# A chunked attention whose instruction order is planned in the kernel, with 16x16 blocks inverted on VectorE and merged on TensorE

## The chip, the cores and the metric

The kernel runs on one core of one Trainium2 chip. The metric is device time in microseconds (us) of one execution. TensorE (PE in the profile) multiplies matrices, VectorE (DVE), ScalarE (ACT) and GpSimd (POOL) work on elements, and SyncE (SP) only issues transfers (DMAs). Each of these takes its own instructions strictly in the order in which the program lists them.

## The reference

The first half is a linear attention with a state per batch and head; the second is a mixture of eight experts on its output.

```python
def _attn_ref(r, k, v, w, a, b):          # each 4 x 8 x 768 x 40 (batch, head, time, channel)
    for t in range(S):
        y[:, :, t] = einsum('bhd,bhde->bhe', rt, state)
        Sa = einsum('bhde,bhe->bhd', state, at)
        state = state * wt[:, :, None, :] - einsum('bhd,bhe->bhde', Sa, bt) + einsum('bhd,bhe->bhde', vt, kt)

def _moe_ref(x, w_gate, w1, w2):          # x = y as 3072 tokens x 320
    P = exp(x @ w_gate - max); eight rounds of normalising rows and columns of P
    out = sum over the 8 experts e of P[:, e] * (relu(x @ w1[e]) @ w2[e])
```

## The kernel before

**Attention.** Time is cut into 12 chunks `c` of 64 steps; `b` is the batch, and the eight heads stand as four pairs (`NP = 4`). There are 48 (chunk, batch) pairs. For each there is a *preparation* (`prep`), which does not depend on the state: two scans on VectorE (`q` L123, `gf` L133), products with them on GpSimd (`kb` L147, `ab` L153 and L154), the matrix of the chunk's inner products on TensorE (`ll` L159), a transpose (`kt` L167), and copies into a set of operands (`sx`, `bb`, `cc`; 20 sets, named `sx` or `st` in the profile).

Then a 64x64 unit triangular matrix per head must be *inverted*. The negated lower part of `ll` goes to DRAM (`ld`) and comes back with one (batch, head, half) on each partition (`load_lu`, L360). Two chunks make a group, so 128 matrices of 32x32 stand on the 128 partitions. VectorE inverts their 8x8 diagonal blocks by rows (`inv_diag`, L184 and L187) and then doubles the block twice, from 8 to 16 and from 16 to 32 (`inv_off` and `contract`: a multiply at L193 and a reduction at L196). `finish` writes the 32x32 inverses to DRAM, `tload` brings them back with the right layout, and `tmat` joins two 32x32 inverses to the 64x64 inverse `tt` with two products on TensorE (`gp` L241, `op` L246).

The *step* (`recur`) is the part that runs through time: for each (c, b) the products `av` (L268), `xc` (two halves, L276), `pu` with `tt` (L287), `c2` (L294; named `c` in the profile), between them the masks and sums on VectorE (`f` L269, `pm` L289, `ws` L296) and copies on ScalarE, then the new state `z` (L311), its transpose `zt` (L316), and the output `y` on GpSimd (L300), which goes to DRAM as `xd`, and to the router as `lp` (L326) and `lg` (L330). A chunk's step of batch b needs the state of the chunk before; the four batches are independent of each other.

**Order.** The function sorts a list of events `(time, function)` with hand-set times (`SKEW`, `P0`, `PD`, `INV_DT`) and writes the code in that order; a scheduler that simulates a timeline then places the instructions of each engine. It does so for the experts' first blocks too, up to `N_MAN = 8`; from there the written order holds.

**Experts.** Each block multiplies 384 tokens with a quarter of an expert's first layer by a seven-product scheme (`product`, L564) and then its second layer (L629). Before the first block, `prep_w` must split and combine the weights (GpSimd and ScalarE) and `prep_x` the tokens read back from `xd` (`xs`; VectorE `xt` L536 to L541, `xcl` and `xch` L544 to L552). The first block needs three `prep_x` units.

Of the kernel before, what the change touches and what calls it, by code (L numbers as in the profile page):

```python
# [3 lines left out]

# [25 lines left out]
def attention(ctx, tc, d, xd, ps, pq, pt, gs, lg):  # L30
    nc = tc.nc
    pin = ctx.enter_context(tc.tile_pool(name="a_in", bufs=1))
    inv = ctx.enter_context(tc.tile_pool(name="a_inv", bufs=1))
# [30 lines left out]
    tt_b = [const.tile([128, 4 * NP, 128], F32, name=f"tt{i}") for i in range(NTB)]
    td_b = [const.tile([128, 4 * NP + 1, 32], F32, name="td")]
    lg_b = [const.tile([128, 4 * NP, 64], F32, name="lg")]
    ab_b = [pin.tile([128, NP, 128], F32, name=f"ab{i}") for i in range(2)]
    kb1 = pin.tile([128, NP, 2, 64], F32, name="kb")
    f_b = [const.tile([128, NP, 2, 104], F32, name=f"f{i}") for i in range(NFB)]
    rb_b = [io.tile([128, NP, 128], F32, name=f"rb{i}") for i in range(NRB)]  # L70
    x1_b = [const.tile([128, NP, 128], F32, name=f"x1{i}") for i in range(2)]
    g1_b = [pin.tile([RP, NP, 65], F32, name=f"g1{i}") for i in range(1)]
    vz_b = [const.tile([128, NP, 104], F32, name=f"vz{i}") for i in range(5)]
    c1_b = [const.tile([R2, NP, 104], F32, name=f"c1{i}") for i in range(2)]
    unf = inv.tile([128, 1056], F32, name="un")
    luf = inv.tile([128, 1056], F32, name="lu")
    prf = inv.tile([128, 2048], F32, name="pr")
    gtf = inv.tile([128, 256], F32, name="gt")
    un, lu, tn = (t[:, 0:1024].rearrange("u (a b) -> u a b", b=32) for t in (unf, luf, prf))
    und, lud = (t.rearrange("u (b x) -> u b x", x=264)[:, :, 0:256].rearrange("u b (c j) -> u b c j", j=32)  # L80
                for t in (unf, luf))
    for t in g1_b + ab_b:
        nc.vector.memset(t, 0.0)

    def clear():
        nc.gpsimd.memset(unf, 0.0)
        nc.gpsimd.memset(unf[:, 0:1024:33], 1.0)
        for t in vz_b + c1_b + lg_b:
            nc.vector.memset(t, 0.0)
        for t in rb_b + f_b:  # L90
            nc.vector.memset(t[96:128], 0.0)
        nc.vector.memset(td_b[0][:, 4 * NP], 0.0)
        for t in x1_b:
            nc.vector.memset(t[:, :, 104:128], 0.0)
        nc.vector.memset(kb1[96:128], 0.0)
        for t in tt_b:
            nc.gpsimd.memset(t, 0.0)
    fresh = set(range(NSX))

    def first_use(i):  # L100
        if i in fresh:
            fresh.discard(i)
            nc.gpsimd.memset(bb_b[i], 0.0)
            nc.scalar.copy(out=sx_b[i][64:128].rearrange("r p h x -> r (p h) x")[:, :, 64:104],
                           in_=cst[64:128, 360:400].unsqueeze(1).broadcast_to([64, 8, 40]))

    state = {"sx": 0, "ab": 0, "g1": 0, "vz": 0, "c1": 0, "tt": 0, "f": 0, "rb": 0, "x1": 0}

    def rot(key, lst):
        i = state[key]  # L110
        state[key] = (i + 1) % len(lst)
        return lst[i]

    zp = [None] * NB

    def prep(c, b, ld):
        cb = c * NB + b
        inp = raws[IN_MAP[cb]][0:RP, 0:1029] if IN_MAP.get(cb) else pin.tile([RP, 1029], F32, name="inp", bufs=2)
        nc.sync.dma_start(out=inp, in_=d["inp"][c, b])
        kb_in = inp[0:R2, 261:773].rearrange("r (p k t) -> r p k t", p=NP, k=2)  # L120
        a_in = inp[0:R2, 773:1029].rearrange("r (p t) -> r p t", p=NP)
        qf = pin.tile([RP, NP, 65], F32, name="q")
        nc.vector.tensor_tensor_scan(  # L123
            out=qf.rearrange("r p t -> r (p t)"), data0=inp[:, 0:260], data1=one65,
            initial=0.0, op0=ALU.mult, op1=ALU.add)
        q = qf[0:R2]
        g1 = rot("g1", g1_b)
        nc.vector.reciprocal(out=g1[:, :, 64], in_=qf[:, :, 64])
        sx = rot("sx", sx_b)
        i = next(j for j in range(NSX) if sx_b[j] is sx)  # L130
        bb, cc = bb_b[i], cc_b[i]
        gf = pin.tile([RP, NP, 65], F32, name="gf", bufs=2)
        nc.vector.tensor_tensor_scan(  # L133
            out=gf.rearrange("r p t -> r (p t)")[:, 259::-1], data0=inp[:, 260:0:-1],
            data1=g1.rearrange("r p t -> r (p t)")[:, 259::-1], initial=0.0, op0=ALU.mult, op1=ALU.add)
        gd[c, b] = dr1.tile([RP, 260], F32, name=f"gd{cb}")
        nc.sync.dma_start(out=gd[c, b], in_=gf.rearrange("r p t -> r (p t)"))
        g = gf[0:R2, :, 64:0:-1]
        if cb < NKB:
            raw = raws[KB_SETS[cb % len(KB_SETS)]]  # L140
            kb = raw[0:R2, 0:512].rearrange("r (p k t) -> r p k t", p=NP, k=2)
            lt = raw[0:64, 512:1024].rearrange("r (p k t) -> r p k t", p=NP, k=2)
        else:
            kb = kb1
            lt = pin.tile([64, NP, 2, 64], F32, name="lt")
        eng = nc.vector if cb < NFAST else nc.gpsimd
        (nc.gpsimd if cb in KB_POOL else eng).tensor_tensor(  # L147
            out=kb[0:R2], in0=kb_in,
            in1=q[:, :, 63::-1].unsqueeze(2).broadcast_to([R2, NP, 2, 64]), op=ALU.mult)
        ab = rot("ab", ab_b)  # L150
        first_use(i)
        nc.gpsimd.tensor_copy(out=cc, in_=q[:, :, 64])
        eng.tensor_tensor(out=ab[0:40, :, 0:64], in0=a_in[0:40], in1=g[0:40], op=ALU.mult)  # L153
        eng.tensor_tensor(out=ab[64:104, :, 64:128], in0=a_in[64:104], in1=g[64:104], op=ALU.mult)  # L154
        nc.scalar.copy(out=sx[64:128, :, 0, 0:64], in_=ab[0:64, :, 0:64])
        nc.scalar.copy(out=sx[64:128, :, 1, 0:64], in_=ab[64:128, :, 64:128])
        ll = pq.tile([128, NP, 2, 64], F32, name="ll", tag="pq")
        for p in range(NP):
            nc.tensor.matmul(ll[:, p], lhsT=kb[:, p], rhs=ab[0:kb.shape[0], p], start=True, stop=True)  # L159
        if cb < NKB:  # L160
            nc.scalar.activation(out=lt, in_=ll[64:128], func=AF.Copy, scale=-1.0)
            (nc.sync if cb < N_SP else nc.scalar).dma_start(out=ld[GRP[c][1], :, b], in_=lt)
            kt = pt.tile([128, NP, 2, 64], F32, name="kt", tag="pt")
        else:
            kt = pq.tile([128, NP, 2, 64], F32, name="kt", tag="pq")
        for p in range(NP):
            nc.tensor.transpose(kt[:, p].rearrange("s h x -> s (h x)")[:, 0:R2],  # L167
                                kb[0:R2, p].rearrange("r k s -> r (k s)"), ident[0:R2, 0:R2])
        nc.vector.tensor_tensor(
            out=sx[0:64, :, :, 0:64], in0=ll[0:64],  # L170
            in1=mask_u.unsqueeze(1).unsqueeze(1).broadcast_to([64, NP, 2, 64]), op=ALU.mult)
        if cb >= NKB:
            nc.scalar.activation(out=lt, in_=ll[64:128], func=AF.Copy, scale=-1.0)
# [646 lines left out]
```

## Time and profile before

| | us |
|---|---|
| three runs: median (lowest to highest) | 1845.69 (1838.58 to 1847.31) |
| the profiled execution | 1846.42 |
| its span, first to last instruction | 1844.6 |
| TensorE busy in the span | 1717.9 |
| VectorE busy | 1395.4 |
| GpSimd busy | 882.4 |
| ScalarE busy | 855.9 |

The profile's rows give for each group of instructions the line in the kernel, the engine, the tiles written and read, the shape, the number of instructions, and busy time and mean. A float32 matmul shows as two records, a transpose as one. Matmuls are pipelined, so what a burst of them costs TensorE is read from one burst's start to the next one's start. The span has two stages: the attention up to about 520 us, and the experts from there.

### The profile page before, as it was taken

How to read it: one execution, taken by the hardware profiler on the slowest of the kernel's cores; microseconds unless marked ns; L12 is line 12 of the kernel's file. 1: busy time of each engine (PE TensorE's matmuls, PEld its weight loads, DVE VectorE, ACT ScalarE, POOL GpSimd, SP SyncE). 2: the span in 40 equal slices, each digit the busy share in tenths (PEclk: the TensorE clock that was granted, in tenths of full speed). 3: DMA queues.
4: the chain of work that ended last, by engine and by line, in shares of the span. 5: the costliest groups of instructions: out<-in, count | busy, mean ns of one | idle time of the engine just before them, and what ended most of it. 6: DMA issues, size and time to landing. Idle time of an engine off the chain costs nothing.

```text
span 1844.6 us, 31499 instructions
## 1 busy us (share of the span) xinstructions
PE 1717.9 (93%) x11843; PEld 1684.3 (91%) x11843; DVE 1395.4 (76%) x2315; ACT 855.9 (46%) x1848; POOL 882.4 (48%) x848
## 2 busy tenths in 40 slices
PE   4478898888989999999999999999999999999999
PEld 4368788888878999999999999999999999999999
DVE  7877979777598868677776868977686877767675
ACT  6357576675643534344343433445343443425342
POOL 6545655441573618355371826007191744628170
PEclk8579899999999999999999999999999999999999
DMA  8477787885730102011110202201020111102001
GB/s 211 117 169 160 175 201 178 178 179 129 188 95 31 56 2 74 21 55 38 38 56 19 75 20 68 66 12 57 20 75 20 56 38 38 57 19 75 5 34 43
DMA packets 194957, 145.10 MB, mean 79 GB/s; under 512 B 143861, under 2 KB 171637, under 8 KB 194805
## 3 DMA queue, kind: packets, MB, share of 16 engines
q1 hardware_dynamic: 191125, 137.35, 28.6%
q10 hardware_dynamic: 3680, 5.74, 1.1%
q8 instruction: 94, 1.54, 0.4%
q14 instruction: 58, 0.48, 0.1%
HBM read 117.00 MB, written 26.04 MB: 78 GB/s over the span
## 4 chain that ended last, share of the span: by engine, by line
PE 72%; DVE 13%; DMA 4%; issue 3%; POOL 3%; ACT 1%; SPq 1%; DVEq 0%; ACTq 0%; POOLq 0%
PE op L629 36%; PE p L564 33%; DVE pr L193 2%; DVE gt L196 2%; DMA inp<-in_inp_dram 1%; DVE un L196 1%; DVE q L123 1%; POOL kb L147 1%; DVE gf L133 1%; PE xc L276 1%; PE ll L159 1%; DMA ld<-lt 1%; DMA xs<-xd 1%; POOL ab L154 1%; DVE sm L582 1%
## 5 line engine op out<-in xcount | busy, mean ns | idle before, releaser
L564 PE MATMUL p<-xch,wh 128*128 128x384 f32 (+1 forms) x1792 | 604.8, 339 | 9.5 <-DVE sm L582 5.6
L585 ACT ACTIVATE hh<-sm 128x384 fp32r<-128x384 f32 x512 | 269.4, 527 | 723.2 <-DVE sm L582 723.2
L629 PE MATMUL op<-wh,hh 128*128 128x320 f32 x1536 | 476.4, 311 | 1.0 <-ACT hh L585 0.9
L629 PE MATMUL op<-wl,hh 128*128 128x320 f32 x1536 | 474.2, 309 | 0.0
L629 PE MATMUL op<-wh,hl 128*128 128x320 f32 x1536 | 466.7, 309 | 0.8 <-DVE hl L588 0.8
L510 POOL TENSOR_TENSOR wl<-ws,wh 128x640 fp32r<-128x640 f32 x60 | 103.1, 1718 | 605.6 <-ACT wh L508 605.4
L588 DVE SCALAR_TENSOR_TENSOR hl<-sm,hh 128x384 fp32r<-128x384 f32 x512 | 373.4, 763 | 2.4 <-ACT hh L585 2.0
L564 PEld LDWEIGHTS p<-xch,wh 128*128 128x128 f32 (+1 forms) x1792 | 336.8, 188 | 13.7 <-DVE sm L582 6.8
L564 PE MATMUL p<-xcl,wh 128*128 128x384 f32 x896 | 302.2, 337 | 0.0
L564 PE MATMUL p<-xch,wl 128*128 128x384 f32 x896 | 301.5, 337 | 0.0
L629 PEld LDWEIGHTS op<-wh,hh 128*128 128x128 f32 x1536 | 289.9, 189 | 1.6 <-ACT hh L585 1.5
L629 PEld LDWEIGHTS op<-wl,hh 128*128 128x128 f32 x1536 | 290.7, 189 | 0.0
L629 PEld LDWEIGHTS op<-wh,hl 128*128 128x128 f32 x1536 | 286.4, 188 | 1.2 <-DVE hl L588 1.0
L582 DVE TENSOR_TENSOR sm<-p,u 128x384 f32<-128x384 f32 x384 | 233.0, 617 | 8.8
L582 DVE TENSOR_TENSOR sm<-p,p 128x384 f32<-128x384 f32 x128 | 71.3, 557 | 129.0 <-PE p L564 74.4
L564 PEld LDWEIGHTS p<-xcl,wh 128*128 128x128 f32 x896 | 168.4, 188 | 0.0
L564 PEld LDWEIGHTS p<-xch,wl 128*128 128x128 f32 x896 | 168.4, 188 | 0.0
L582 DVE TENSOR_TENSOR p<-p,p 128x384 f32<-128x384 f32 x128 | 71.1, 556 | 101.6 <-PE p L564 101.2
L582 DVE TENSOR_TENSOR u<-p,p 128x384 f32<-128x384 f32 x128 | 70.8, 553 | 57.2 <-PE p L564 56.0
L159 PE MATMUL ll<-ab,kb 128*128 128x128 f32 x336 | 60.8, 335 | 48.3 <-POOL ab L154 23.2
L518 POOL TENSOR_TENSOR wl<-ss,wh 128x512 fp32r<-128x512 f32 x60 | 89.7, 1495 | 30.1 <-ACT wh L515 25.9
L159 PEld LDWEIGHTS ll<-ab,kb 128*128 128x128 f32 x336 | 52.3, 237 | 54.1 <-POOL kb L147 27.2
(161 smaller groups left out, 2747.3 us busy)
## 6 DMA issues: line engine op xcount, KB each, us to landing
ws<-in_wts_dram SPq DMA_DIRECT2D x60, 832.0 KB
inp<-in_inp_dram SPq DMA_DIRECT2D x42, 450.2 KB
rb<-in_r_dram SPq DMA_DIRECT2D x48, 224.0 KB
gd<-gf SPq DMA_DIRECT2D x48, 113.8 KB
gr<-gd SPq DMA_DIRECT2D x48, 113.8 KB
vz<-in_v_dram SPq DMA_DIRECT2D x48, 112.0 KB
ld<-lt ACTq DMA_DIRECT2D x40, 128.0 KB
f<-in_vt_dram SPq DMA_DIRECT2D x48, 80.0 KB
```

Of the source, the lines that this page charges most:

```text
L123: nc.vector.tensor_tensor_scan(out=qf.rearrange("r p t -> r (p t)"), data0=inp[:, 0:260], data1=one65, initial=0.0, op0=ALU.mult, op1=ALU.add)
L133: nc.vector.tensor_tensor_scan(out=gf.rearrange("r p t -> r (p t)")[:, 259::-1], data0=inp[:, 260:0:-1], data1=g1.rearrange("r p t -> r (p ...
L159: nc.tensor.matmul(ll[:, p], lhsT=kb[:, p], rhs=ab[0:kb.shape[0], p], start=True, stop=True)
L193: nc.vector.tensor_tensor(out=prv, in0=a.unsqueeze(3).broadcast_to([nu, n_c, n_k, n_r]), in1=m.unsqueeze(1).broadcast_to([nu, n_c, n_k, n_ ...
L196: nc.vector.tensor_reduce(out=dst, in_=prv.rearrange("u c k r -> u c r k"), op=ALU.add, axis=AX.X)
L510: g.tensor_tensor(out=wl[:, 0:640], in0=raw[:, 256:896], in1=wh[:, 0:640], op=ALU.subtract)
L518: g.tensor_tensor(out=lv[:, 3:7], in0=so[:, :, 0], in1=hv[:, 3:7, 0], op=ALU.subtract)
L564: nc.tensor.matmul(o, lhsT=w_, rhs=x_, start=(j == 0), stop=(j == 3))
L582: eng.tensor_tensor(out=out, in0=x, in1=y, op=ALU.add)
L585: nc.scalar.activation(out=hh[:, f, h], in_=sm[f][:, h], func=AF.Relu)
L588: v.scalar_tensor_tensor(out=hl[:, f, h], in0=sm[f][:, h], scalar=0.0, in1=hh[:, f, h], op0=ALU.max, op1=ALU.subtract)
L629: nc.tensor.matmul(ops[i], lhsT=a[:, h, cs], rhs=w_[:, cw], start=(f == 0 and h == 0 and j == 0), stop=(last and h == 1 and j == 2))
```

## The change

1. **The order.** A class `Plan` collects every operation of the attention (on TensorE, VectorE, ScalarE, GpSimd and SyncE) with a duration, what it depends on, a due time, and the buffers that it takes and gives back. `order()` plays them through, engine by engine, always taking the ready operation with the earliest key, and the code is written in that order under a manual schedule. All eight PSUM banks become one pool. Transfers that ScalarE issued (`ld`) go to SyncE.
2. **The inversion.** VectorE stops at 16x16 blocks. Blocks are merged from 16 to 32 and from 32 to 64 on TensorE by products of 32-row tiles (`merge`: `mm_ga`, `mm_at`, `mm_tb`, `mm_gb`, `mm_tc`).
3. **The groups.** The first chunk is inverted alone; the groups are 1, 2, 2, 2, 2, 2, 1 chunks.
4. **The step.** `tt` is stored as two 64-wide halves and not as a block-diagonal 128x128 matrix, so `pu` and `c2` are two 64-row products for each pair of heads. `xd` has its rows in another order, which `_layout` follows.

The experts' code is the same.

```diff
+    def order(self):
+        ...
+                    busy[e] = o.end = t + d
+        ...
-GROUPS = [[0, 1], [2, 3], [4, 5], [6, 7], [8, 9], [10, 11]]
-NSX = 20
-T_LEAD = 2
+SIZES = dict(set=17, inp=3, q=2, gf=2, g1=2, kb=2, ab=2, lt=2, vz=5, rb=2, gr=2, f=3, x1=2, c1=2, pm=2, ws=2, y=2,
+             z=5, tt=2, inv=1, m_a=1, m_d=1, m_l=1, m_g=1, m_t=1, m_h=1, ps=8)
+PACE = 7.0
+LEAD = 40.0
+GROUPS = ((0,), (1, 2), (3, 4), (5, 6), (7, 8), (9, 10), (11,))
-    INV = [(inv_diag, (i,)) for i in range(1, 8)] + [(inv_off, a) for a in ((0, 8, 8), (16, 8, 8), (0, 16, 8))]
+        for i in range(1, 8):
+            ...
+                V.tensor_tensor(out=prv, in0=und[0:nu, :, 0:i, 0:i],
+                                in1=lud[0:nu, :, 0:i, i].unsqueeze(2).broadcast_to([nu, 4, i, i]), op=ALU.mult)
+                V.tensor_reduce(out=und[0:nu, :, 0:i, i], in_=prv, op=ALU.add, axis=AX.X)
+        for i in range(2):
+            un_, lu_ = un[0:nu, i], lu[0:nu, 16 * i:16 * i + 16, 16 * i:16 * i + 16]
+            for k, (dst, a, m) in enumerate(((gt, un_[:, 0:8, 0:8], lu_[:, 0:8, 8:16]),
+                                             (un_[:, 0:8, 8:16], gt, un_[:, 8:16, 8:16]))):
+                for n, f in enumerate(mul_add(dst, a, m)):
+                    o = P.add("DVE", (0.75, 1.1)[n], f, [o])
+        def mm_ga():
+            for g in range(16):
+                for r in quarter:
+                    nc.tensor.matmul(B(b_ga, 16, 32)[r, g], lhsT=lp16[r, g], rhs=at16[r, g], start=True, stop=True)
+        ...
+        p1 = P.add("PE", 2.4, mm_ga, la, acq=[b_ga, t_g], rel=[t_a])
+        e1 = P.add("ACT", 0.64, lambda: A.copy(out=gt16, in_=B(b_ga, 16, 32)), [p1], rel=[b_ga])
+        p2 = P.add("PE", 1.2, mm_at, [e1] + ldd, acq=[b_at, t_t], rel=[t_g, t_d])
-            nc.tensor.matmul(pu[:, p], lhsT=tts[c][:, b * NP + p], rhs=x1[:, p], start=True, stop=True)
+                for h in halves:
+                    nc.tensor.matmul(wide(b_pu)[h, p], lhsT=tt_b[t_tt.slot][h, b * NP + p], rhs=X1()[h, p],
+                                     start=True, stop=True)
-    for _, fn, args in sorted(ev, key=lambda x: x[0]):
-        fn(*args)
+    with tc.manual_schedule(engines={E_.PE, E_.DVE, E_.Activation, E_.Pool, E_.SP}):
+        for o in P.order():
+            o.fn()
```

What the change moves is seen in the order in which instructions stand on an engine (line, operation, written and read tiles, shape). The line numbers of the changed kernel are its own: L386 and L388 are the row-wise inversion, L358 and L360 multiply and reduction of the block doubling, L279 and L286 the scans, L332 the mask into the operand set, L398 the transposed copy.

VectorE, from the first doubling on, in the first group, before (128 partitions, two chunks; the copy comes only after a second doubling with up to 2048 products at a time):

```order
L193 TENSOR_TENSOR pr<-un,lu 128x512
L196 TENSOR_REDUCE gt<-pr 128x64
L123 SCALAR_TENSOR_TENSOR q<-inp,cst 112x260
L193 TENSOR_TENSOR pr<-gt,un 128x512
L128 RECIPROCAL g_215<-q 112x4
L196 TENSOR_REDUCE un<-pr 128x8x8
L133 SCALAR_TENSOR_TENSOR gf<-inp,g_215 112x260
L193 TENSOR_TENSOR pr<-un,lu 128x512
L169 TENSOR_TENSOR sx_166<-ll,cst 64x8x64
L196 TENSOR_REDUCE gt<-pr 128x64
L193 TENSOR_TENSOR pr<-gt,un 128x512
L196 TENSOR_REDUCE un<-pr 128x8x8
```

The same place now (64 partitions, one chunk):

```order
L358 TENSOR_TENSOR pr<-un,lu 64x512
L360 TENSOR_REDUCE gt<-pr 64x64
L358 TENSOR_TENSOR pr<-gt,un 64x512
L360 TENSOR_REDUCE un<-pr 64x8x8
L332 TENSOR_TENSOR st_110<-bk_84,cst 64x8x64
L358 TENSOR_TENSOR pr<-un,lu 64x512
L360 TENSOR_REDUCE gt<-pr 64x64
L358 TENSOR_TENSOR pr<-gt,un 64x512
L360 TENSOR_REDUCE un<-pr 64x8x8
L286 SCALAR_TENSOR_TENSOR gf_92<-inp_88,g_94 112x260
L332 TENSOR_TENSOR st_111<-bk_83,cst 64x8x64
L398 COPY tn<-un 64x256
```

The second doubling, from 16 to 32, is gone from VectorE, and the copy `tn` follows at once.

TensorE, where the first chunk's inverse is put together, before:

```order
L159 MATMUL ll<-ab_205,kb 128x128 x4
L167 MATMUL kt<-cst,kb 128x104 x4
L246 MATMUL op<-td,lg 64x64 x8
L241 MATMUL gp<-td,lg 64x64 x8
L287 MATMUL pu<-x_213,tt_201 128x128 x4
L276 MATMUL xc_989<-f_209,sx_180 104x104 x4
```

Now (L325 is `ll`, L330 `kt`; `bk` are the PSUM banks):

```order
L330 MATMUL bk_79<-cst,kb_96 128x104 x4
L437 MATMUL bk_81<-a_149,l_148 32x32 x64
L325 MATMUL bk_80<-ab_98,kb_96 128x128 x4
L330 MATMUL bk_79<-cst,kb_97 128x104 x4
L443 MATMUL bk_81<-g_150,d_151 32x32 x32
L449 MATMUL bk_80<-d_151,g_150 32x64 x32
L457 MATMUL bk_81<-a_153,l_154 64x32
L457 MATMUL bk_82<-a_153,l_154 64x32
```

In the place of 32 products of 64x64 for each chunk stand 224 products of 32 or 64 columns, in five bursts of which each waits for a copy of the one before.

VectorE, from the attention to the experts, before:

```order
L550 TENSOR_TENSOR xcl_5426<-xt,xch_5425 128x4x128
L552 TENSOR_TENSOR xch_5425<-xt,xch_5425 32x4x128
L289 TENSOR_TENSOR pm<-pu,cst 128x416
L330 COPY lg<-lp 128x8
L536 TENSOR_TENSOR xt<-xs 128x256
L537 TENSOR_TENSOR xt<-xs 128x256
L540 TENSOR_TENSOR xt<-xs,xt 128x256
L541 TENSOR_TENSOR xt<-xs,xt 128x256
L269 TENSOR_TENSOR f_210<-av,cst 104x8x64
L296 TENSOR_TENSOR ws<-c_5288,c_222 104x416
```

Now (L558 is `pm`, L568 `ws`, L613 `lg`, L746 to L751 `xt`):

```order
L558 TENSOR_TENSOR pm_135<-bk_79,cst 128x416
L568 TENSOR_TENSOR ws_137<-bk_79,c_134 104x416
L558 TENSOR_TENSOR pm_135<-bk_80,cst 128x416
L568 TENSOR_TENSOR ws_137<-bk_79,c_133 104x416
L613 COPY lg<-bk_79 128x8
L855 TENSOR_REDUCE mxs<-lg 128x1
L746 TENSOR_TENSOR xt<-xs 128x256
L747 TENSOR_TENSOR xt<-xs 128x256
L750 TENSOR_TENSOR xt<-xs,xt 128x256
L751 TENSOR_TENSOR xt<-xs,xt 128x256
```

Before, the experts' `prep_x` stood between the last steps; now all of it stands behind the last `lg` of the attention, and the same holds of the experts' first work on ScalarE, GpSimd and TensorE.

More of the change, by code (lines that the diff above doesn't have):

```diff
@@ L3 @@
 from functools import partial
+from heapq import heappop, heappush
 import numpy as np
@@ L39, in attention, with many @@
-    dr1 = ctx.enter_context(tc.tile_pool(name="a_dr1", bufs=1, space=bass.MemoryType.DRAM))
+    dr = ctx.enter_context(tc.tile_pool(name="a_dr", bufs=1, space=bass.MemoryType.DRAM))
+    def many(pool, n, shape, name):
+        return [pool.tile(shape, F32, name=f"{name}{i}") for i in range(n)]
     cst = const.tile([128, 64 + 64 + 104 + 128 + 40 + 260], F32, name="cst")
-    nc.sync.dma_start(out=cst, in_=d["cst"])
     mask_u = cst[0:64, 0:64]
@@ L64, in attention @@
[L64 to L173, printed above, removed]
-        nc.scalar.copy(out=sx[0:64, :, :, 64:104], in_=kt[0:64, :, :, 0:40])
-        nc.scalar.activation(out=bb[0:64, :, 0:40], in_=kt[64:128, :, 0, 0:40], func=AF.Copy, scale=-1.0)
-        nc.scalar.activation(out=bb[64:128, :, 64:104], in_=kt[64:128, :, 1, 0:40], func=AF.Copy, scale=-1.0)
-        if cb >= NKB:
-            (nc.sync if cb < N_SP else nc.scalar).dma_start(out=ld[GRP[c][1], :, b], in_=lt)
-        return dict(cc=cc, sx=sx, bb=bb)
@@ new lines, in attention @@
+    inv = [[dr.tile([2, 64, NB, NP, 2, 64], F32, name=f"ld{s}"), dr.tile([128, 16, 16], F32, name=f"dd{s}"),
+            dr.tile([128, 16, 16], F32, name=f"ad{s}")] for s in range(len(GROUPS))]
+    group = {c: (s, i) for s, g in enumerate(GROUPS) for i, c in enumerate(g)}
+    ready_by = [0.0] * (NCH * NB)
+    for j in reversed(range(NCH * NB)):
+        g = GROUPS[group[j // NB][0]]
+        ready_by[j] = NB * g[0] * PACE - LEAD - (NB * (g[-1] + 1) - 1 - j) * PACE
+        if j + 1 < NCH * NB:
+            ready_by[j] = min(ready_by[j], ready_by[j + 1] - FIRST)
@@ new lines, in attention, with clear @@
+    halves = [slice(64 * h, 64 * h + 64) for h in range(2)]
+    def clear(eng, e, dur, t, v=0.0, deps=()):
+        return P.add(eng, dur, lambda: e.memset(t, v), deps)
+    o_cst = P.add("SP", 0.5, lambda: nc.sync.dma_start(out=cst, in_=d["cst"]), move=1.5)
+    z_g1 = [clear("DVE", V, 0.3, t) for t in g1_b]
+    z_kb = [clear("DVE", V, 0.3, t[96:128]) for t in kb_b]
+    z_ab = [clear("DVE", V, 0.5, t) for t in ab_b]
+    z_vz = [clear("DVE", V, 0.45, t) for t in vz_b]
+    z_c1 = [clear("DVE", V, 0.45, t) for t in c1_b]
@@ new lines, in attention @@
+    z_rb = [clear("POOL", G, 0.5, t[96:128]) for t in rb_b]
+    z_f = [clear("POOL", G, 0.8, t[96:128]) for t in f_b]
+    z_y = [clear("POOL", G, 0.5, t[96:128]) for t in y_b]
+    z_un = clear("POOL", G, 0.6, unf)
+    z_un = clear("POOL", G, 0.3, unf[:, 0:544:17], 1.0, deps=[z_un])
+    z_lp = clear("POOL", G, 0.6, lp32)
+    z_dg = []
+    for k, r in enumerate(quarter):
+        one = ident[r, r].unsqueeze(1).broadcast_to([32, 16, 32])
+        for t in (lp16[r], at16[r]) + ((gt32[r, :, 32:64],) if k % 2 else ()):
+            z_dg.append(P.add("ACT", 0.62, lambda t=t, one=one: A.copy(out=t, in_=one), [o_cst]))
@@ L356, in load_lu, with inverse @@
+    solved, o_dd, o_ad = {}, {}, {}
+    def inverse(s):
+        ld, dd, ad = inv[s]
+        n = len(GROUPS[s])
+        nu = 64 * n
+        t_inv = Token("inv", 2)
+        loads = []
         for cc in range(n):
@@ L376, in attention @@
+    for s, chunks in enumerate(GROUPS):
+        for c in chunks:
+            for b in range(NB):
+                prep(c, b)
+        inverse(s)
+        for c in chunks:
+            merge(c)
+    for b in range(NB):
+        load_v(0, b)
     for c in range(NCH):
         for b in range(NB):
-            for k in range(5):
-                ev.append((5 * c + k + SKEW * b, step, (c, b)))
-        t = 5 * c + 2 - T_LEAD
-        ev.append((t - L_LEAD, tload, (c,)))
-        for half in range(2):
-            ev.append((t + 2 * SKEW * half, tmat, (c, half)))
```

694 lines of the change are left out of this document (459 added, 235 removed).

## The prediction

> **What bounds the kernel now.** I read the page's head, then a table of windows by stage, to see which stage the change can touch.
>
> ```profile
> span 1844.6 us, 31499 instructions
> PE 1717.9 (93%) x11843; PEld 1684.3 (91%) x11843; DVE 1395.4 (76%) x2315; ACT 855.9 (46%) x1848; POOL 882.4 (48%) x848
> ...
> core 0: us, PE busy (x) PEld busy (x) DVE busy (x) ACT busy (x) POOL busy (x), PEclk, DMA share, GB/s
> 0.00:115.00 115.00, 55.68 (x329) 50.58 (x329) 86.08 (x145) 55.65 (x137) 64.42 (x90) 0.67 0.67 163
> 115.00:400.00 285.00, 246.05 (x2298) 229.99 (x2297) 238.34 (x346) 192.56 (x486) 164.32 (x184) 0.95 0.79 179
> 400.00:440.00 40.00, 38.15 (x379) 35.17 (x378) 32.96 (x48) 23.76 (x61) 7.02 (x12) 1.00 0.57 124
> 520.00:560.00 40.00, 33.57 (x199) 31.60 (x197) 37.25 (x55) 18.97 (x36) 29.52 (x27) 0.96 0.27 87
> 560.00:1844.00 1284.00, 1275.85 (x8004) 1272.01 (x8003) 951.96 (x1649) 516.55 (x1020) 581.48 (x500) 1.00 0.13 42
> ```
>
> From 560 us on TensorE is busy 1275.85 of 1284 us, in code that does not change. All that can be won lies ahead of 520 us. There I read by tile when the first inversion starts and ends, when the steps run, and from the timeline when the last sum `ws` starts:
>
> ```profile
> L184 DVE TENSOR_TENSOR pr<-un,lu x42: 165/335/1183, 55.1 to 411.8; 128x4 f32<-128x4 f32 x6, 128x16 f32<-128x16 f32 x6, 128x36 f32<-128x36 f32 x6, 128x64 f32<-128x64 f32 x6
> L349 DVE COPY pr<-un x6: 999/1046/1272, 96.7 to 445.5; 128x1024 f32<-128x1024 f32 x6
> L289 DVE TENSOR_TENSOR pm<-pu,cst x48: 548/582/621, 115.3 to 517.5; 128x416 f32<-128x416 f32 x48
> 519.53 0.59 DVE L296 TENSOR_TENSOR ws<-c,c 104x416 f32<-104x416 f32 x1 [0.23 <-PE c L294]
> by line: issue 12.5%; DVE pr L193 7.3%; DMA inp<-in_inp_dram 7.2%; DVE gt L196 7.1%; POOL kb L147 5.6%; DVE q L123 5.6%; DVE un L196 5.4%; DVE gf L133 4.4%; PE xc L276 3.7%; PE ll L159 3.6%; POOL z L311 2.9%; POOL ab L154 2.7%; POOL ab L153
> ```
>
> The attention has three terms: 115.3 us until the first step reaches `pm`; 47 steps of (517.5 - 115.3) / 47 = 8.56 us each; 2 us to the last `ws` at 519.5, behind which stand 1844.6 - 519.5 = 1325.1 us. The last row is the chain of waits from 115 to 400 us: no engine owns it, but inversion (L193, L196) has 20% of it and TensorE's lines stand low. So VectorE's inversion, coming in lumps, holds the steps back, not TensorE's throughput.
>
> **What a step costs TensorE.** In this stretch bursts follow each other without idle time, so the price of a burst is the distance between starts:
>
> ```profile
> 319.73 1.08 PE L159 MATMUL ll<-ab,kb 128*128 128x128 f32 x8
> 320.64 0.52 PE L167 MATMUL kt<-cst,kb 104*128 104x104 f32 x4
> 321.00 0.90 PE L276 MATMUL xc<-f,sx 128*104 128x104 f32 x8
> 321.73 1.04 PE L268 MATMUL av<-rb,vz 128*104 128x128 f32 x8
> 322.70 1.14 PE L241 MATMUL gp<-td,lg 64*64 64x64 f32 x16
> 323.77 0.54 PE L316 MATMUL zt<-cst,z 104*40 104x104 f32 x4
> 324.15 0.90 PE L294 MATMUL c<-pm,bb 128*104 128x104 f32 x8
> 324.88 1.08 PE L159 MATMUL ll<-ab,kb 128*128 128x128 f32 x8
> 325.79 1.06 PE L287 MATMUL pu<-x,tt 128*128 128x128 f32 x8
> 326.69 0.53 PE L276 MATMUL xc<-f,sx 128*104 128x104 f32 x4
> 327.14 1.14 PE L246 MATMUL op<-td,lg 64*64 64x64 f32 x16
> 328.22 1.34 PE L276 MATMUL xc<-f,sx 128*104 128x104 f32 x12
> 514.22 1.06 PE L326 MATMUL lp<-gs,y 104*128 104x8 f32 x8
> ```
>
> `ll` 0.91, `kt` 0.36, `xc` 0.73 for each half, `av` 0.97, of which about 0.1 goes with the turn to 64-row products behind it (0.87 is taken), `gp` 1.07, `zt` 0.38, `c` 0.73, `pu` 0.90, `op` 1.08. `lp` is 1.06 by its own row, tail included; 0.9 is taken, half of that for a step. A step with its preparation is then 0.91 + 0.36 + 1.46 + 0.87 + 0.38 + 0.73 + 0.90 + 0.45 = 6.06, a chunk 4 x 6.06 + 2 x 2.15 = 28.5 us, of 4 x 8.56 = 34.2: TensorE is 83% used.
>
> **Inversion on VectorE (removed, the largest cut).**
>
> ```profile
> L196 DVE TENSOR_REDUCE un<-pr 128x64 f32<-128x512 f32 (+2 forms) x24 | 47.9, 1996 | 0.1
> L196 DVE TENSOR_REDUCE gt<-pr 128x64 f32<-128x512 f32 (+2 forms) x24 | 45.8, 1908 | 0.2
> L193 DVE TENSOR_TENSOR pr<-un,lu 128x512 f32<-128x512 f32 (+2 forms) x24 | 31.0, 1294 | 0.1
> L193 DVE TENSOR_TENSOR pr<-gt,un 128x512 f32<-128x512 f32 (+2 forms) x24 | 30.5, 1271 | 0.1
> L184 DVE TENSOR_TENSOR pr<-un,lu 128x4 f32<-128x4 f32 (+6 forms) x42 | 14.9, 355 | 15.7 <-DMA lu<-ld 14.9
> L187 DVE TENSOR_REDUCE un<-pr 128x4 f32<-128x4 f32 (+6 forms) x42 | 9.9, 235 | 0.9
> ...
> L196 DVE TENSOR_REDUCE gt<-pr 128x64 f32<-128x512 f32 x12 | 12.9, 1071 | 0.1
> L193 DVE TENSOR_TENSOR pr<-gt,un 128x512 f32<-128x512 f32 x12 | 9.4, 786 | 0.1
> ```
>
> Doublings now take 155.2 us and rows 24.8, in six groups 30 us each. What stays is the first doubling: 4 x (0.73 + 1.07) = 7.2 us, with rows of 24.8 / 6 = 4.1 us and a copy of a quarter of 1.05 us: 11.6 a group, seven groups 81 us (a group of one chunk costs the same, since the free size is the same). VectorE loses some 100 us, all of it in stages where it was 83% busy, so from here it does not bound. TensorE is late next.
>
> **Merges on TensorE (added).** No row shows a 32-row product. A chunk has 64 + 32 + 64 + 32 + 32 = 224 products, 448 records, in the place of 64 records for 4.3 us. In the rows above a record costs (0.73 / 8) 92 ns at 104 columns, and 58 ns at 64 (the 1.07 less 0.14 for the turn, by 16); it goes by columns. Upper end: 58 ns each, 26 us a chunk. Lower end: half of it for 32 columns, 29 ns, and four quarters at once, 7 ns, 3.2 us. I take 20 ns, 9.0 us: most products have 32 columns (29 ns), and quarters that lie in different rows can share some time. **`pu` and `c2`** are 16 records of 104 columns in two halves each: 0.74 if the halves run together, 1.47 if one after the other; I take 0.74, since the halves share neither rows nor output partitions. A step with preparation becomes 6.06 - 1.63 + 1.48 = 5.91.
>
> [...]
>
> **The start (moved).** The first inversion waits for four preparations and not eight, but the same eleven scans stand ahead of it on VectorE. Ends: 55.1 (the scans set it) and 55.1 x 4 / 8 = 28 (the preparations do); I take 48, nearer to the first, since the scans are the same. Then 11.6 + 2.4 (a scan and two masks between) gives 62, and from the copy to the first `pm` 18.6 us now, 20 with three more bursts and copies in line: the first `pm` at 82 (72 to 92).
>
> **The steps.** By 82 us 16 preparations and one merge are done. Left for TensorE: 48 x (5.91 - 1.27) + 32 x 1.27 + 11 x 9.0 = 223 + 41 + 99 = 363 us. The best window above, 400 to 440, has it 95% busy; with the lumps gone from VectorE I take that: 363 / 0.95 = 382, or 8.1 us a step. Gain: 33 us at the start, 20 in the steps.
>
> **The hand-over (moved, a cost).** Before, the three `prep_x` ran between the last steps; now they stand behind the last `lg`.
>
> ```profile
> 470.00:515.00 45.00, 14.70 (x18) 3.71 (x6) 0.15 (x1) 0.96 0.68 186
> L547 DVE TENSOR_TENSOR xch<-xs,xch 32x384 fp32r<-32x384 f32 x3 | 3.0, 1013 | 0.1
> L544 DVE TENSOR_TENSOR xcl<-xs,xch 128x384 fp32r<-128x384 f32 x3 | 1.7, 553 | 0.7 <-ACT xch L538 0.6
> ```
>
> The first row is the window with the instructions on `xt` alone, VectorE first: 14.70 + 3.0 + 1.7 = 19.4 us. The first product needs all but some 2.5 of it, and 2 us pass from the last `ws` over `y` and `lp` to `lg`. TensorE had done 2.6 us of products by 519.5 and was idle 6.4 us in 520 to 560, of which I let 3 fall away: 19 us lost. GpSimd's work on the weights runs beside it.
>
> **SyncE** issues 640 transfers and not some 535 (ScalarE's 40 `ld` are among them), 53 a chunk:
>
> ```profile
> L360 SPq DMA_DIRECT2D lu<-ld x48: 302/482/1769, 36.0 to 404.7; - x48
> ```
>
> At 0.48 us each that is 26 us of 32 a chunk: hidden, if a transfer that waits does not hold the loads queued behind it. Data fall: the blocks written back are a quarter. The rest (pools, row order of `xd`, clearing) hides behind the transfers of the first inputs; without that cover a few us.
>
> **Sum**, against the profiled execution: 82 + 382 + 2 + 19 + 1325.1 = 1810.1, and 1.8 us outside the span: 1812. The profiled time, 1846.42, lies 0.7 us above the median, so it is compared as it is.
>
> **Rivals.**
> - *The products do not run side by side* (slower). At 29 ns a merge is 13 us, `pu` and `c2` 1.47: 48 x 1.46 + 11 x 4 = 114 us more, by 0.95 120: 1932. For it: no row shows two products at once. Against: different rows and outputs. It decides from (1845 - 1812) x 0.95 = 31 us of added TensorE time on. 10%.
> - *Each turn between tile shapes drains TensorE* (no change). The rows show 0.1 to 0.14 us at both turns of `gp`. Two bursts a step and five a merge are 96 + 55 = 151 bursts at 0.24: 36 us, by 0.95 38: 1850. [...] For it: the turns are measured. Against: bursts of the same shape often stand side by side in the new order. 17%.
> - [...] 15%.
> - *The planned order does not hold* (slower): transfers land later than planned (`inp` has 7% of the chain), SyncE stands, and steps keep 8.56 + 0.6 us: 82 + 430 + 2 + 19 + 1327 = 1860. 8%.
>
> **How the numbers follow.** My sum has 50%. A measurement of this kernel can tell about 0.5%, 9 us. Faster by more: nearly all of the sum's cases, the cheap merges, some of the turns: 0.66. Same: most of the turns: 0.16. Slower: 0.18. The range, 1766 to 1860, leaves out the serial products and about half of the cheap merges.
>
> **What would show it.** Right: first `pm` near 82, VectorE's inversion near 81 us, TensorE over 90% busy between 90 and 460 with VectorE under 75%, and some 19 us of idle TensorE ahead of the first product. Wrong: a merge far from 9 us, `pu` bursts of 1.5 us, or idle TensorE in the steps with SyncE named as what ended it.

## The result, and the profile after

| | before | changed |
|---|---|---|
| median of 4 runs | 1843.4 us | 1907.1 us |
| range | 1838.6 to 1847.3 | 1899.1 to 1912.0 |
| profiled execution, its span | 1846.4, 1844.6 | 1907.2, 1905.4 |

The changed kernel is slower: ratio 1.034, 95% interval 1.030 to 1.039; the forecast was 1812 us. First the head of the changed kernel's page (busy us and share of the span), then its instructions on `pm` and `ws` (duration in ns, first and last start), the windows of three stages, and the chain of waits from 115 to 520 us by line:

```profile
span 1905.4 us, 42341 instructions
PE 1769.6 (93%) x17219; PEld 1721.7 (90%) x17219; DVE 1311.2 (69%) x2278; ACT 865.1 (45%) x1845; POOL 834.0 (44%) x856
```

```profile
L558 DVE TENSOR_TENSOR pm<-bk,cst x48: 565/592/593, 89.4 to 535.7; 128x416 f32<-128x416 f32 x48
L568 DVE TENSOR_TENSOR ws<-bk,c x48: 558/592/593, 91.5 to 537.4; 104x416 f32<-104x416 f32 x48
```

```profile
core 0: us, PE busy (x) PEld busy (x) DVE busy (x) ACT busy (x) POOL busy (x), PEclk, DMA share, GB/s
89.40:535.70 446.30, 393.90 (x8256) 360.68 (x8256) 230.01 (x427) 257.75 (x634) 145.97 (x212) 0.90 0.58 129
537.40:564.00 26.60, 1.07 (x9) 0.98 (x9) 15.71 (x17) 9.17 (x14) 19.88 (x19) 0.57 0.48 157
564.00:640.00 76.00, 62.81 (x327) 56.80 (x328) 61.17 (x104) 30.45 (x61) 39.64 (x38) 0.86 0.22 69
```

```profile
by line: PE bk L541 15.4%; PE bk L530 9.9%; PE bk L565 8.2%; PE bk L555 8.1%; issue 8.0%; PE bk L325 6.3%; PE bk L449 6.2%; PE bk L464 5.0%; PE bk L610 4.3%; PE bk L581 3.5%; DMA inp<-in_inp_dram 3.5%; PE bk L330 3.3%; PE bk L457 3.1%; PE b
```

The same window of before, between its first and last `pm`:

```profile
115.30:517.50 402.20, 349.97 (x3297) 327.31 (x3296) 317.58 (x466) 263.84 (x654) 205.73 (x231) 0.95 0.74 173
```

The start won 25.9 us (first `pm` 89.4, not 115.3). The 47 steps lost 44.1 (446.3, not 402.2). Behind the last `ws` stand 1905.4 - 537.4 = 1368.0 us, 42.9 more than before. Together 60.8 us. The chain has changed hands: VectorE's inversion is gone from its head and TensorE's lines lead, with "issue" in fifth place. The stretch has two losses in one row: TensorE was idle for 446.3 - 393.9 = 52.4 us, and its granted clock was 0.90. The trace has the clock as 1.00 or 0.50, the shortest piece at either 3.41 us long (308.83 to 312.24 at 0.50, 312.24 to 315.65 at 1.00): 85 us at half clock, where before had 38.

Where the idle time lies is read from TensorE's groups between 89 and 536 us; behind the bar stand busy time, mean ns, idle time ahead and what ended it. Two pieces of the timeline show one such gap and what a burst costs:

```profile
L449 PE MATMUL bk<-d,g 32*32 32x64 f32 x1408 | 33.8, 248 | 16.1 <-issue 15.7 <-ACT c L548 0.2
L464 PE MATMUL bk<-tt,g 32*64 32x32 f32 x704 | 23.2, 220 | 0.0
L457 PE MATMUL bk<-a,l 32*64 32x32 f32 x704 | 16.3, 239 | 8.4 <-issue 6.6 <-ACT a L469 1.3 <-DVE st L332 0.4
L437 PE MATMUL bk<-a,l 32*32 32x32 f32 x1408 | 16.1, 194 | 2.9 <-issue 1.7 <-DMA a<-ad 1.3
L443 PE MATMUL bk<-g,d 32*32 32x32 f32 x704 | 10.3, 204 | 6.5 <-issue 6.5
```

```profile
196.76 1.48 PE L457 MATMUL bk<-a,l 32*64 32x32 f32 x48
198.17 0.42 PE L449 MATMUL bk<-d,g 32*32 32x64 f32 x4
201.92 1.91 PE L449 MATMUL bk<-d,g 32*32 32x64 f32 x60 [3.33 <-issue]
...
302.38 1.29 PE L437 MATMUL bk<-a,l 32*32 32x32 f32 x128
303.60 0.93 PE L565 MATMUL bk<-pm,st 64*64 64x104 f32 x16
304.46 0.57 PE L330 MATMUL bk<-cst,kb 104*128 104x104 f32 x4
```

All five lines are merge products, and 30.5 us of idle time ahead of them ended in "issue": TensorE waited for nothing that the profile shows. The gap at 198 us stands *inside* a burst, between its fourth and fifth record. The page has a queue for instructions, whose packets rise with TensorE's records:

```profile
q8 instruction: 135, 2.21, 0.5%
```

That is 135 packets of 16 KB for 17219 records of products and as many weight loads (before: 94 for 11843). By division that is 64 bytes for each and 128 records with their loads in a packet, an estimate. In the trace each of the 15 "issue" gaps that are longer than 1 us ends 1.3 to 2.0 us after such a packet landed. Hence the first theory: TensorE ran out of instructions.

### The profile page after: what moved, and what is told of

It reads as the page before. It is cut to its first block, busy times and chain, and to the rows that moved or that the text cites. A ratio compares the mean times of both kernels' runs of the same rounds, so it can differ in the third digit from the quotient of the medians.

```text
span 1905.4 us, 42341 instructions
## 1 busy us (share of the span) xinstructions
PE 1769.6 (93%) x17219; PEld 1721.7 (90%) x17219; DVE 1311.2 (69%) x2278; ACT 865.1 (45%) x1845; POOL 834.0 (44%) x856
## 3 DMA queue, kind: packets, MB, share of 16 engines
q8 instruction: 135, 2.21, 0.5%
## 4 chain that ended last, share of the span: by engine, by line
PE 86%; DVE 6%; issue 3%; DMA 3%; SPq 1%; ACT 1%; POOL 0%; DVEq 0%; POOLq 0%; ACTq 0%
PE op L839 35%; PE p L774 32%; PE bk L541 4%; PE bk L530 2%; PE bk L325 2%; PE bk L555 2%; PE bk L565 2%; PE bk L449 2%; PE bk L464 1%; PE bk L610 1%; DMA inp<-in_inp_dram 1%; DMA xs<-xd 1%; PE bk L581 1%; PE bk L330 1%; PE bk L457 1%
## 5 line engine op out<-in xcount | busy, mean ns | idle before, releaser
L798 DVE SCALAR_TENSOR_TENSOR hl<-sm,hh 128x384 fp32r<-128x384 f32 x512 | 369.0, 754 | 3.1 <-ACT hh L795 2.6
L595 POOL TENSOR_TENSOR y<-ws,gr 104x256 f32<-104x256 f32 x48 | 37.7, 785 | 156.0 <-DVE ws L568 128.2
L310 POOL TENSOR_TENSOR ab<-inp,gf 40x256 f32<-40x256 f32 x88 | 67.8, 770 | 81.8 <-DVE gf L286 46.4
```

Source lines behind the costliest of these rows:

```text
L310: (V if fast and not h else G).tensor_tensor(out=AB()[r, :, 64 * h:64 * h + 64], in0=I()[r, 773:1029].rearrange("r (p t) -> r p t", p=NP), ...
L798: v.scalar_tensor_tensor(out=hl[:, f, h], in0=sm[f][:, h], scalar=0.0, in1=hh[:, f, h], op0=ALU.max, op1=ALU.subtract)
```

## The experiments

Each ratio is against the kernel before on the same chip, with its 95% interval; the changed kernel has 1.034 (1.030 to 1.039).

**Merges spread out.**
```diff
-        p1 = P.add("PE", 2.4, mm_ga, la, acq=[b_ga, t_g], rel=[t_a])
+        p1 = few(2.4, mm_ga, 16, 4, la, [b_ga, t_g], [t_a])     # a chain of pieces of 16 products, each "heavy"
...
+                    if o.heavy and t < room - 1e-9:             # in Plan.order
+                        held.append((k, i, o))
...
+                        room = t + SPACE                        # 1.2 us
```


> The changed kernel with the same products, cut into pieces of 32 records (16 products) that the plan sets at least 1.2 us apart, so that ordinary bursts stand between them. Instruction theory (TensorE runs out of instructions in a merge's row of small products, since the next 16 KB arrive only every 4 us or so; the 27 gaps that end in 'issue' cost some 30 us, and the half clock that follows costs more): the gaps go, 30 us, and half clock in the steps falls from 85 us towards 40, another 15 to 20: 1855 to 1870. Rival (the products of 32 rows, or each turn between tile shapes, cost what they cost wherever they stand): nothing gained, and with three times as many turns some 10 us lost: 1905 to 1920. Rival (a merge's delay holds up the steps): slower too, since each merge now takes longer from first product to last.

1.017 (1.014 to 1.020), 28 us faster than the changed kernel. Its window from the first to the last `pm`, and its group of `tb`:

```profile
93.70:511.80 418.10, 395.76 (x8242) 355.70 (x8241) 225.91 (x417) 255.44 (x630) 144.94 (x211) 0.94 0.61 135
```

```profile
L464 PE MATMUL bk<-d,g 32*32 32x64 f32 x1408 | 30.5, 225 | 1.7 <-DVE st L338 1.6
```

Between the first and the last `pm`, the gaps that ended in "issue" fell from 31.3 us to 2.0 (those over 1 us: from 28.6 us in 15 to none), and half clock from 85 to 49 us. Both falls are larger than what one execution differs from the next: in "tiny", "warm" and "rows32" below, whose attention is the changed kernel's own, such gaps took 14 to 27 us and half clock 68 to 103. The same products, with more turns between shapes, cost less: the turns are not the cause.

**A row of small products by itself.**
```diff
         for o in P.order():
             o.fn()
+        for i in range(40):
+            for g in range(4):
+                for r in quarter:
+                    nc.tensor.matmul(bank[0][r, 32 * g:32 * g + 32], lhsT=cst[r, 232:264], rhs=cst[r, 264:296], ...)
```


> The changed kernel with 640 useless 32x32 products (1280 records, four row quarters in turn, as in the merge's first product) in one row at the same place, where TensorE waits for nothing. Instruction theory: the first one or two hundred records run at the merge's 10.8 ns, then the row runs at the pace at which instructions arrive, 128 records per 4 us: about 40 us in all, in clumps of 128 with gaps between them that no semaphore ends. Rival (a merge's gaps come from semaphores, from the transfers around it or from its changes of tile): 1280 x 10.8 ns = 14 us without gaps.

One run, its timeline on TensorE:

```profile
550.06 2.88 PE L635 MATMUL bk<-cst 32*32 32x32 f32 x198 [0.26 <-DVE lg L613]
556.24 1.73 PE L635 MATMUL bk<-cst 32*32 32x32 f32 x128 [3.29 <-issue]
559.71 1.93 PE L635 MATMUL bk<-cst 32*32 32x32 f32 x128 [1.74 <-issue]
563.18 1.93 PE L635 MATMUL bk<-cst 32*32 32x32 f32 x128 [1.54 <-issue]
...
580.81 1.93 PE L635 MATMUL bk<-cst 32*32 32x32 f32 x128 [1.54 <-issue]
584.28 1.01 PE L635 MATMUL bk<-cst 32*32 32x32 f32 x58 [1.54 <-issue]
```

After 198 records TensorE runs in clumps of 128, 3.47 us apart (one after 3.75): in this row instructions arrive at 27 ns a record. Each of these clumps starts 1.3 to 1.5 us after a packet of 16 KB landed. An `xc` record takes 92 ns and so asks for fewer than arrived here; the first merge burst wants one every 9.5 ns (128 records in 1.22 us above). This shows the first theory.

**Two rows of useless products in the hand-over.**
```diff
+        for i in range(100):      # "warm"
+            nc.tensor.matmul(bank[0][:, 0:128], lhsT=ident, rhs=ident, ...)
...
+        for i in range(36):       # "rows32"
+            nc.tensor.matmul(bank[0][0:32, 0:512], lhsT=cst[0:32, 232:264], rhs=cst[0:32, 0:512], ...)
```


> The changed kernel with 100 useless 128x128 fp32 products (200 records, 23 us at full clock) on TensorE between the last lp and the first product of the experts, where it was idle for 24 us. Clock theory (idle time costs twice: 34 us of half clock follow it): the clock stays full through the hand-over and the first 40 us behind it, 15 to 17 us gained: 1890. Rival (the half clock there has another cause, the waits of the first expert blocks): no change, 1900 to 1912, or slower by what the useless products overrun.

> The changed kernel with 36 useless products of 32 rows and 512 columns (72 records) on TensorE between the last lp and the experts, where 100 products of 128 rows ran at full clock after the first few us. Activity theory (the clock of each window of 3.4 us follows from how many rows times columns were streamed in the window before; 32 rows count a quarter): TensorE is busy without a gap there and yet at half clock, a record takes 0.73 us, the row 50 us. Rival (the clock follows from the busy share): full clock after the first window, 0.37 us a record, 28 us. The run's end says nothing by itself, since the experts' pools wait for these products.

"warm" took 1928 us (1.045): its price says nothing, for the products read `cst`, whose pool the experts' tiles must wait for, and the first product moved from 564.0 to 583.1. But a window of "warm" and one of "rows32" show what the clock did (the granted clock is the third number from the end):

```profile
545.00:565.00 20.00, 20.00 (x180) 19.91 (x179) 0.84 (x3) 0.00 (x0) 0.00 (x0) 1.00 0.03 7
```

```profile
535.00:592.00 57.00, 57.00 (x68) 11.42 (x66) 1.52 (x4) 0.00 (x0) 0.00 (x0) 0.50 0.05 13
```

Both are busy without a gap. With 128 rows the granted clock is 1.00, with 32 rows 0.50 for 57 us on end (the row took 58.2 us, 0.81 for each of its 72 records, of which the trace has 68; 0.73 was expected). In the changed kernel itself TensorE was busy without a gap from 479.49 to 489.73 us, in `lp`, `av`, `pu`, `zt` and `c2`, at 0.50. So the busy share alone does not account for the clock. That it follows rows times columns stays the author's estimate: the two rows of useless products also differ in the columns streamed (128 and 512) and in their weight columns (128 and 32), and no run changes one of these alone.

**Narrower products; then more work on top.**
```diff
-    lhsT=gt32[r, g], rhs=TT()[r, g, 32:64]            # tc: 64 weight columns; gb alike
+    lhsT=gt32[r, g, 0:32], rhs=TT()[r, g, 32:64]
-    lhsT=gt16[r, i * 8 + g], rhs=d16[r, i * 8 + g]    # tb: 64 columns streamed
+    lhsT=gt16[r, g], rhs=d16[r, g, k % 2 * 32:k % 2 * 32 + 32]
...
+            nc.tensor.matmul(bank[t.slot], lhsT=fb[:, 0:128], rhs=fb, ...)   # "filler", four a chunk, 512 columns
```


> The spread kernel with narrower merge products of the same number (448 records a chunk): tb streams the 32 columns that are not zero (64 before), and gb and tc load 32 weight columns (64 before), since the other half of their output is zero or already there; the copies follow by quarters, five more a chunk, two of them on VectorE. In the changed kernel's rows 64 records of tb took 1.39 us, of gb 1.86, of tc 1.98, and of at, with 32 columns on both sides, 0.99: 3 us of TensorE a chunk less, 33 us in all at full clock. TensorE bound (it is 95% busy in the spread kernel's steps): 25 to 33 us gained, 1846 to 1855. Rival (instructions set the pace there, 128 records in 3.5 us, whatever they do): under 8 us. Rival (ScalarE, with 1.4 us more a chunk, holds the merges): no gain or a loss.

> The narrow kernel with four useless products a chunk added on TensorE (128 rows, 512 columns, bf16, one record each; 0.22 to 0.43 us), each ahead of at, gb (two) and tc, into the bank that the products behind it overwrite: 48 products, 10 to 20 us more work. In the narrow kernel 74 us of the steps ran at half clock, often fully busy with few rows. Activity theory (a window of 3.4 us is granted half the clock when the window before streamed too few rows times columns): half clock in the steps falls to 50 us or less, 12 us or more won back, so that 10 to 20 us more work cost nothing: 1880 to 1892. Rival (the clock follows the idle time, which stays): half clock at 70 us or more and the whole price paid: 1898 to 1908.

"narrow": 1.023 (1.021 to 1.025), 0.6% *slower* than "spread" with less work on TensorE. "filler": 1.022 (1.018 to 1.026), the same. The windows from first to last `pm` of "narrow" and, with its useless products, of "filler":

```profile
95.10:517.30 422.20, 382.85 (x8251) 344.02 (x8249) 239.41 (x440) 271.66 (x663) 148.63 (x211) 0.91 0.59 134
```

```profile
96.10:521.30 425.20, 383.88 (x8296) 336.88 (x8294) 240.55 (x441) 271.93 (x663) 148.11 (x211) 0.94 0.59 133
```

```profile
L453 PE MATMUL bk<-fb x48: 376/379/634, 74.2 to 509.1; 128*128 128x512 bf16 x48
```

Of TensorE's busy time a part ran at half clock; counting that part half (an estimate: in the changed kernel `xc` records start 92 ns apart at 1.00 and 173 at 0.50) gives the work at full clock:

| between the first and the last `pm`, us | length | work at full clock | lost to the clock | idle |
|---|---|---|---|---|
| before | 402 | 333 | 17 | 52 |
| changed | 446 | 359 | 35 | 52 |
| "spread" | 418 | 372 | 24 | 22 |
| "narrow" | 422 | 348 | 34 | 39 |
| "filler" | 425 | 360 | 24 | 41 |

Narrowing saved 24 us of work and lost more than that again: 11 us to the clock, since half clock rose from 49 to 74 us, and 17 us of idle time. Only the third theory allowed a loss, and the idle time that ScalarE ended did rise from 4 to 19 us; none had the clock. The 33 us expected were too many, because rows at half clock were read as if they were at full clock. In the changed kernel the same 64 records of `gb` took 1.06 us in one place (361.00, clock 1.00) and 1.86 in another (281.60, clock 0.50):

```profile
281.60 1.93 PE L457 MATMUL bk<-a,l 32*64 32x32 f32 x64 [1.32 <-ACT a L469]
283.46 2.42 PE L449 MATMUL bk<-d,g 32*32 32x64 f32 x64
...
361.00 1.13 PE L457 MATMUL bk<-a,l 32*64 32x32 f32 x64
362.06 0.46 PE L449 MATMUL bk<-d,g 32*32 32x64 f32 x17
```

The fillers, 48 products of 0.38 us by their own row, brought half clock down to 53 us (50 or less was expected) and left the run time where it was: 12 us more work at full clock, 11 us won back from the clock. The mean clock of all four executions says the same, 0.961 to 0.964 against 0.954 to 0.958 in "narrow". This is what the activity theory had said.

**Other pools for the hand-over.**
```diff
-    tt_b = many(pin, SZ["tt"], [128, 4 * NP, 64], "tt")
+    tt_b = many(const, SZ["tt"], [128, 4 * NP, 64], "tt")
...
+    psets = {i: ctx.enter_context(tc.tile_pool(name=f"a_set{i}", bufs=1)) for i in SET_ORDER}
...
-            pool = x1 if i else x0
+            pool = x1 if i else xc
```


> The changed kernel with other pools alone: tt, the merge's and the inversion's tiles and the sets lie in pools of their own, the dead ones first, and xch, xcl in one of their own. No instruction is added and the plan is the same. Pool theory (the experts' preparation stands behind the last step because its memory lies over the pool that holds tt, used until the last pu at 535.6 us): the first loads of weights and xd move ahead by some 40 us, TensorE's 24 us of idle time ahead of the first product fall to under 8, and of the 34 us of half clock behind it most goes (17 us): 1867 to 1880, with up to 10 us lost again in the last steps for the work on VectorE and ScalarE that now stands there. Rival (the plan written out for all queues keeps everything behind its last instruction): no change, 1900 to 1912.

> The kernel with spread merges, and pools as in the run with other pools, but with the experts' weight tiles (x0) still over a pool that lives to the end, so that no weight cast can stand ahead of the last merge's copies; only xt, xch and xcl can move ahead. By the two single results taken together: steps as in the spread kernel (last ws near 513), behind it 1333 to 1342 in the place of 1362: 1848 to 1860. If the moved xt and xch still hold up the last steps (as they did by 17 us with the weights among them), nothing is left of it: 1870 to 1880. Against the kernel before that is equal to 1.5% slower; faster than it only if the steps too get shorter, which nothing here says.

"hand": 1.030 (1.025 to 1.035), which the time can't tell from the changed kernel. The trace can: the experts' first load, which in the changed kernel goes out at 535.7, as the last `pu` is done, goes out at 460.4, and behind the last `ws` stand 1335.5 us and not 1368.0. So the pools were the cause; but the last `ws` came at 556.7 and not 537.4. Waits of that kernel from 490 to 557 us (us in total, times, longest):

```profile
POOL xt L751 <- DMA xs<-xd: 16.6, 1, 16.6
ACT wh L727 <- POOL ss L721: 6.7, 1, 6.7
PEld bk L558 <- ACT tt L486: 4.4, 1, 4.4
```

The moved work stood ahead of the steps in its engines' queues: `y` behind `xt`, which waited 16.6 us for a transfer, and the last copy to `tt` behind a weight cast, which waited 6.7. "spread_hand", 1.014 (1.013 to 1.016), won 16 us behind the last `ws` of "spread" and lost 12 ahead of it, in the same way (GpSimd's `xt` stood 31.5 us for VectorE's `xch`, with `y` behind it).

**Groups.**
```diff
-GROUPS = ((0,), (1, 2), (3, 4), (5, 6), (7, 8), (9, 10), (11,))
+GROUPS = ((0, 1), (2, 3), (4, 5), (6, 7), (8, 9), (10, 11))                  # "groups"
+GROUPS = ((0,), (1,), (2, 3), (4, 5), (6, 7), (8, 9), (10, 11))              # "lone01"
```


> The changed kernel with the pairs of before, ((0,1),(2,3),...), so that the first chunk is not solved alone. If the lone first chunk is what brings the first pm from 115.3 to 89.4 us: first pm at 105 to 115, six inversions and not seven (12 us less on VectorE, which does not bound), 1920 to 1935. Rival (the earlier first pm comes from the plan's order and the shorter inversion; the lone chunk only moves work that TensorE must do anyway): first pm within 8 us of 89 and the end within 8 us of 1907.

> The changed kernel with the groups ((0,),(1,),(2,3),...,(10,11)): the first chunk still solved alone, but no lone chunk at the end. With the pairs of before the run was 16 us faster than the changed kernel, although its first pm came 9 us later; its steps from the 39th on were 10 us shorter. If the lone last chunk costs that (its inversion ends only some 40 us before the last step): first pm near 89, last steps as with pairs, 1880 to 1890. Rival (the lone first chunk costs it, since the second pair then waits): as with the changed kernel or slower, 1900 to 1915.

"groups": 1.024 (1.022 to 1.025), 16 us faster than the changed kernel; "lone01": 1.038 (1.035 to 1.041). Their first and last `pm`:

```profile
L558 DVE TENSOR_TENSOR pm<-bk,cst x48: 567/592/593, 98.3 to 524.5; 128x416 f32<-128x416 f32 x48
```

```profile
L558 DVE TENSOR_TENSOR pm<-bk,cst x48: 557/592/593, 100.9 to 537.7; 128x416 f32<-128x416 f32 x48
```

The lone first chunk brings the first `pm` 9 us forward, and by the seventh `pm` the lead is 1 us (137.8 against 138.7). With two lone chunks at the start nothing of it is left: the first `pm` of "lone01" came at 100.9 (89 was expected) and the seventh at 158.5. That the lone last chunk costs is not shown, although from the 40th `pm` to the last the changed kernel takes 70 us, "groups" and "lone01" 60 each: "warm", "tiny" and "rows32", with the changed kernel's own attention, take 60, 65 and 61 there, and "spread", which solves the last chunk alone too, 59. Of the 70 us 17 were at half clock in that one execution, 3 in "groups". What makes six groups 16 us faster than seven stays open.

**The plan's order left to the scheduler.**
```diff
-    with tc.manual_schedule(engines={E_.PE, E_.DVE, E_.Activation, E_.Pool, E_.SP}):
-        for o in P.order():
-            o.fn()
+    for o in P.order():
+        o.fn()
```


> The changed kernel whose plan is only the order in which the program is written; the instructions are no longer held to it, and the scheduler orders every queue as it did before the change. Rows: the plan ended at 434 us by its own costs and the chip took 537, and in its order VectorE stood 40 us at q for inp, with the steps' sums queued behind. If the plan's order is a loss against the scheduler's (a rival of mine: it does not hold against late transfers): 1880 to 1895, with the merges' gaps still there. If it is a gain: 1920 to 1960, with steps above 9.5 us.

1.083 (1.079 to 1.087), 2000 us: steps of 11.0 us. For these instructions the plan's order is worth some 90 us against the scheduler's, so leaving the order to the scheduler would have made the change slower still. Whether a third order does better is not tested.

**All together.**
```diff
+GROUPS = ((0,), (1,), (2, 3), (4, 5), (6, 7), (8, 9), (10, 11))   # with "spread", "narrow", measured durations in the plan
+        to = x0.tile([128, 4, 2, 128], F32, name="xt")            # xs and ws early, xt and xch late
```


> Spread and narrow merges, the groups of lone01, the measured durations of the merges, pu and c2 in the plan, and pools that free the experts' staging tiles early, with xt, xch and the weight tiles still over a pool that lives to the end: the loads of xd and weights stand ahead of the end, and no work of another engine can stand in front of the last steps. Summed from the single runs: the spread kernel's 1879, less 25 to 33 (narrow), less 8 to 12 (the first product 12 us behind the last ws in the place of 25), less 0 to 10 (no lone chunk at the end): 1826 to 1846, so faster than before by 0 to 1.2%. If TensorE's products are no longer what bounds once they are narrow, the gains do not add: 1850 to 1860.

1.022 (1.021 to 1.024), 1887 us: the gains did not add. "narrow" and two lone chunks were no gains, and the first product still came 22 us behind the last `ws`. Of the three `xs` that it needs, two were asked for at 421 us, but the third only at 536, 12 us behind the last `ws`, having waited for VectorE's `xt`; ScalarE's and VectorE's work on it followed. No version here beats the kernel before; the nearest, "spread_hand", is 1.4% slower.

## Why the prediction was wrong

- **Inversion on VectorE: right.** 81 us were forecast; 79.9 and 3.4 for the copies were measured, and VectorE no longer bounds. A lone chunk cost nearly what two did: 681 ns a multiply of the doubling and 1063 a reduction, against 756 and 1081.
- **Merges: right in size, in part by luck.** The five groups above are 99.7 us of busy time for 11 chunks, 9.1 each (9.0). But that holds stretches at half clock, which the sum didn't have. Whole bursts at full clock add up to some 7 us a chunk: `ga` 9.5 ns a record (128 in 1.22 us), `at` 8.8, `tb` 16, `gb` 16.6, `tc` 31 (64 in 1.98 us). The mean of 20 that was taken is 15, with a wide spread.
- **`pu` and `c2` side by side: right.** 303.60 to 304.46 is 0.86 us for the 16 records of `c2`; 0.74 was taken, 1.47 feared. Two bursts of `pu` in a row take 1.57.
- **The start: nearly.** 89.4, in the range 72 to 92. The inversion began at 45.6 (48) and its copy stood at 59.9 (62); from there to the first `pm` it took 29.5 us and not 20, with two gaps of the merge in it, 3.6 us. Of the 25.9 us won the lone first chunk has 9: with pairs ("groups") the first `pm` came at 98.3.
- **The steps: wrong, and this is the step that failed.** "363 / 0.95 = 382" became 446. The work was right: 359 us at full clock, as in the table above, and 363 forecast. What failed is the 0.95, which allowed 19 us for everything else: 87 were lost, 52 of them idle and 35 to the clock (before: 52 and 17). It was read off a window with no product of 32 rows in it and a clock of 1.00. Two things were left out. Gaps that ended in "issue" cost 31 us of idle time (the other 21 are near what 0.95 allowed), and in "tiny" instructions arrived at 27 ns a record; and the granted clock was 0.50 for 85 us, of which TensorE was busy 69.
- **The hand-over: half right.** 19 us were forecast and 42.9 lost. From the last `ws` to the first product 26.6 us passed, and behind that 25 us ran at half clock (3 before), some 11 us which the sum had at nothing. Its cause was named wrongly: not the order, but memory pools, of which the one with `tt` has `pu` as its last reader.
- **The rivals.** Cheap merges, after which TensorE would not have bound (15% of the chances), stood on a price that no run shows; the runs showed some 7 us a chunk at full clock, and TensorE still led the chain. Serial products: not `pu` and `c2`, but `tc`, at 31 ns a record, ran no faster than the 29 that the prediction gave to one product after the other; the merges as a whole still took less than the sum had. Turns of the tile: not the cause, by "spread". A planned order that doesn't hold: open in part. VectorE stood 36.7 us at `q` for `inp` in the steps, and waits for `inp` have 3.5% of the chain, 14 us; "free" shows only that the scheduler's order is worse. None of the four has what "spread", "tiny" and "filler" showed, the supply of instructions (31.3 us of gaps, 2.0 in "spread") and the clock (74 us at half, 53 in "filler").

## What to carry to other kernels

Count instructions as well as time: in "tiny" a row of short products ran 198 records and then got one every 27 ns, and with merges of 9 to 31 ns a record the gaps that ended in "issue" fell from 31.3 us to 2.0 when the same products were spread between longer ones. A share of busy time, or the length of a burst, read in one window holds only for that window's instructions and clock; and a stretch of one execution (70 us above) is compared with the same stretch of others before a cause is named for it; before work is cut into tiles of few rows, look at what the clock did wherever few rows were streamed. When memory is shared between stages, look for the pool with the latest last reader (with other pools the experts' first load went out at 460.4 us and not at 535.7), and at what work moved ahead will stand in front of in the queues that it enters (19 us at the last `ws` of "hand", 12 of "spread_hand").
